# Turning x as pairs of fp16 numbers read as fp32: linear attention with a highway layer on one core

## The chip, the cores and the metric

The kernel runs on one core of a Trainium2 chip. Its time is the device time of one execution in microseconds. The median of three runs of the kernel before is 118.87 us (118.81 to 119.09).

The core's engines each work through a queue of their own, in order: TensorE (PE in the profile; PEld are its weight loads), VectorE (DVE), ScalarE (ACT), GpSimd (POOL) and SyncE (SP), which here issues nearly all transfers. TensorE writes to PSUM only. Semaphores order the engines among each other.

## The reference, cut to what matters

```python
# q, k, v: 8 batches x 8 heads x 576 rows x 64, fp32
q_s = softmax(q, axis=-1)                  # over the 64 features
k_s = softmax(k, axis=2)                   # over the 576 rows
kv  = einsum('bhsd,bhse->bhde', k_s, v)    # 64 x 64 for each batch and head
x   = einsum('bhsd,bhde->bhse', q_s, kv)   # then to 4608 rows x 512
H   = maximum(x @ w_h, 0)
T   = 1 / (1 + exp(-(x @ w_t + b_t)))
out = T * H + (1 - T) * x                  # 4608 x 512, fp32
```

## The kernel before, in words

Rows of x are worked in 36 tiles of 128 rows by 512 columns. Two batches make nine tiles: four of each batch alone, and one that holds the last 64 rows of both. Every step of every tile is a small function, and a long list of step names (`ORDER`) written by hand fixes the order in which they are recorded; each engine's queue is that list cut down to its own instructions. A suffix of a step picks its engine (D VectorE, A ScalarE, P GpSimd).

The steps for a batch: load k, v, q; exponentials of k and q in fp16 (`ek`, `eq`, ScalarE); v to fp16 (`vc`); `kv` multiplies k by v for all heads, and `kr`, `kn` divide by the sums; `qt` turns the exponentials of q on TensorE, and `qc` copies them out of PSUM (`qd` turns those of the last batch by DMA).

The steps for a tile i:

- `xu` (L361): q by kv on TensorE, with the row sums, into PSUM.
- `rs`, `x` (L370, L376): VectorE takes reciprocals and writes x, scaled, as fp16 into SBUF (tile x16, 128 x 512).
- `xt` (L384): TensorE turns x into PSUM, because the next matmuls need its columns on the partitions. Here x is the loaded weight and an identity moves through. Four turns of 128 x 128 fp16; turn n takes every second column of a block of 256, so that n = 2c + r holds the columns 256c + 2p + r, p being the partition. The weights w_h and w_t are loaded in the same arrangement of rows (`load_w`).
- `xe` (L391): VectorE or ScalarE copies the turned x, 512 fp16 numbers a partition, into tile xT in SBUF.
- `mh` (L419) and `mt` (L411): four matmuls each of 512 columns; a quarter of xT is the loaded weight, and w_h (halved, less the identity) or w_t moves through. `bw` puts the bias into the gate's PSUM first, by ScalarE (L399) or by a matmul (L401).
- `th` (tanh on ScalarE, L433 and L435), `dd` (L439), `uu` (L453 on VectorE, or L450 and L451 on GpSimd), `oo` (L471, GpSimd) and `st` (store) finish the tile.

Three tiles (0, 4 and 5) go through the first of these steps in two halves; the last tile's gate goes in two halves of columns. The turned x has one place in PSUM, `turned` (one bank, of which the first half is used), so the turns of one tile wait for the copy of the tile before. The same bank, read as fp32 under the name `spare`, is written by the `fill` matmuls (L167) that keep TensorE busy in the first 17 us. `idf` and `idh` are identities in fp32 and fp16; `idf` is there today, since it is taken off w_h.

Of the kernel before, what the change touches and what calls it, by code (L numbers as in the profile page):

```python
# [8 lines left out]
FP32 = mybir.dt.float32  # L9
FP16 = mybir.dt.float16  # L10
# [55 lines left out]
def kernel(  # L66
# [10 lines left out]
    nc = tc.nc  # L77
    B, H, S, D = q.shape
    DM = H * D
    P = 128  # L80
# [12 lines left out]
    xtp = pool("xtp", 3)  # L93
# [10 lines left out]
    idf = consts.tile([P, P], FP32, name="idf")  # L104
    idh = consts.tile([P, P], FP16, name="idh")
    w16 = {w: consts.tile([P, KC, DM], FP16, name="w16" + w) for w in "th"}
# [8 lines left out]
    turned = ps_xt.tile([P, 2, 4, P], FP16, tag="xtps", name="turned")  # L115
    spare = turned.rearrange("p a c d -> p (a c d)").bitcast(FP32)
    T = {}

    def once(name, make):
        if name not in T:  # L120
            T[name] = make()
        return T[name]
# [10 lines left out]
    def heads(i, k):  # L133
        return (k, k + 1) if i in HALVED else (0, 2)
# [6 lines left out]
    def columns(i, h):  # L141
        return slice(PIECES[h], PIECES[h + 1]) if i == LAST else slice(0, DM)

    def gate(i, h):
        return f"tps{i}_{h}" if i == LAST else f"tps{i}"
# [34 lines left out]
    def load_kv(which):  # L180
        def step(e, b, c):
            n = (2 if which == "k" else 1, 2)[b] if b < 2 else 4
            nc.sync.dma_start(landing(which, b)[:, c:c + n], rows_of(which, b)[:, c:c + n])
        return step
# [193 lines left out]

    def xt(e, i, k):
        k0, k1 = heads(i, k)  # L380
        t = T[f"xtps{i}"] = turned[:, 0]
        for n in range(2 * k0, 2 * k1):
            n0 = n // 2 * 2 * P
            nc.tensor.matmul(t[:, n], T[f"x{i}"][:, n0 + n % 2:n0 + 2 * P:2], idh, is_transpose=True,  # L384
                             start=True, stop=True, skip_group_check=True)

    def xe(e, i, k):
        k0, k1 = heads(i, k)
        t = once(f"xT{i}", lambda: xtp.tile([P, 4, P], FP16, tag="xT", name=f"xT_{i}"))
        copy = nc.vector.tensor_copy if e == "D" else nc.scalar.copy  # L390
        copy(t[:, 2 * k0:2 * k1], T[f"xtps{i}"][:, 2 * k0:2 * k1])  # L391


    def bw(e, i, h=0):
# [8 lines left out]
    def parts_of(i, k):  # L403
        return range(2 * k, 2 * k + 2) if i in HALVED else range(4)

    def mt(e, i, k):
        cs = columns(i, k)
        parts = parts_of(i, k)
        first = once(f"mt{i}", lambda: k) == k and len(parts) < 4
        for n in parts:  # L410
            nc.tensor.matmul(T[gate(i, k)][:, cs], T[f"xT{i}"][:, n], w16["t"][:, n, cs], start=False,  # L411
                             stop=(n == parts[-1] and not first), skip_group_check=True)

    def mh(e, i, k):
        first = f"gps{i}" not in T
        t = once(f"gps{i}", lambda: ps_g.tile([P, DM], FP32, tag="gps", name=f"gps_{i}"))
        parts = parts_of(i, k)
        for n in parts:
            nc.tensor.matmul(t, T[f"xT{i}"][:, n], w16["h"][:, n], start=(first and n == parts[0]),  # L419
                             stop=(n == parts[-1] and not (first and len(parts) < 4)), skip_group_check=True)  # L420


# [50 lines left out]
    def st(e, i, h):  # L473
# [22 lines left out]
        k=load_kv("k"), v=load_kv("v"), q=load_q, w=load_w, b=load_b, bp=bp, bc=bc,  # L496
        wtc=wt_cast, whc=wh_cast, whd=wh_less_identity, ek=ek, vc=vc, kv=kv, kr=kr, kn=kn, eq=eq, qt=qt, qc=qc, qd=qd,
        xu=xu, rs=rs, x=x, xt=xt, xe=xe, bw=bw, mt=mt, mh=mh, th=th, dd=dd, uu=uu, oo=oo, st=st)
    with tc.manual_schedule():
        for step in ORDER.split():  # L500
            name, _, eng = step.partition(":")
# [32 lines left out]
```

## Time and profile before

| | |
|---|---|
| median of the runs | 118.87 us |
| span of the profiled execution | 116.9 us |
| between the two | 2.0 us |
| mean granted TensorE clock | 0.995 |
| HBM read, written | 30.41 MB, 9.44 MB |

The profiled execution's time is known as its span, from the first to the last instruction; the median of the runs counts what lies around it too. In the profile a row of a group reads: line, engine, operation, output and inputs by the program's names, shapes, count; then busy time and the mean of one in ns; then the idle time of the engine just before them, and what ended it. A matmul's record holds its whole passage through the array, and records of matmuls that follow each other overlap; their spacing is read from the chain of waits, which takes each piece from where the one before it ends. The chain goes back from the last instruction, at each step to what released it.

### The profile page before, as it was taken

The page shows a single profiled execution, that of the slowest core. Times are in us where ns is not written, and L with a number is a line of the kernel's source. Part 1 is how long each engine was busy: PE and PEld are TensorE (multiplying, and loading weights), DVE is VectorE, ACT ScalarE, POOL GpSimd, SP SyncE. Part 2 cuts the span into 40 slices and gives each one's busy share as a digit, 9 for nine tenths or more (in the row PEclk, how much of TensorE's full clock was granted, in tenths as well). Part 3 has the DMA queues.
Part 4 walks back from the last instruction along what each step waited for, and adds up shares of the span by engine and source line. Part 5 has one row for each costly group of instructions (what it writes and reads, how often), then busy time and mean ns, then how long its engine had stood idle before and what let it go on. Part 6 is the DMA issues. An engine that isn't in the chain of part 4 may idle for free.

```text
span 116.9 us, 3424 instructions
## 1 busy us (share of the span) xinstructions
PE 109.5 (94%) x1351; PEld 61.6 (53%) x1351; DVE 93.3 (80%) x222; ACT 90.0 (77%) x132; POOL 89.1 (76%) x99
## 2 busy tenths in 40 slices
PE   5999987999999999999999999999999999999930
PEld 2354544545665656565665547566564555554520
DVE  5642587589799979979889798988989887899870
ACT  4356461897999999989999999998597998545520
POOL 5022237208996999999999999999989699999960
PEclk9999999999999999999999999999999999999998
DMA  2999999999999999999999999999999956992875
GB/s 42 399 392 377 408 398 385 375 377 379 393 391 397 383 391 393 358 375 387 357 376 360 387 392 363 390 381 383 399 398 217 302 204 270 397 404 115 315 295 179
DMA packets 24195, 40.58 MB, mean 347 GB/s; under 512 B 5362, under 2 KB 11762, under 8 KB 24180
## 3 DMA queue, kind: packets, MB, share of 16 engines
q1 hardware_dynamic: 24032, 40.24, 96.9%
q8 instruction: 10, 0.16, 0.6%
q10 hardware_dynamic: 148, 0.14, 0.4%
q14 instruction: 5, 0.04, 0.1%
HBM read 30.41 MB, written 9.44 MB: 341 GB/s over the span
## 4 chain that ended last, share of the span: by engine, by line
PE 67%; POOL 15%; issue 6%; DVE 5%; DMA 3%; SPq 1%; POOLq 0%; DVEq 0%
PE tps L411 18%; PE gps L419 16%; PE turned L167 9%; POOL o L471 7%; PE xu L361 6%; PE turned L384 5%; PE kv L269 5%; PE qps L324 4%; POOL u L451 4%; DMA out_dram<-o 3%; POOL g L450 2%; PE qps L319 2%; POOL v L259 2%; DVE x L376 2%; PE tps L401 1%
## 5 line engine op out<-in xcount | busy, mean ns | idle before, releaser
L471 POOL TENSOR_TENSOR o<-u,x 128x512 f32<-128x512 f16 (+1 forms) x36 | 40.6, 1143 | 1.6 <-DVE u L453 0.7
L411 PE MATMUL tps<-w16t,xT 128*128 128x512 f16 (+1 forms) x148 | 37.3, 373 | 0.0
L419 PE MATMUL gps<-w16h,xT 128*128 128x512 f16 x144 | 36.8, 379 | 0.5 <-DVE xT L391 0.5
L376 DVE TENSOR_TENSOR x<-xu,rs 128x512 f16<-128x512 f32 (+1 forms) x39 | 25.2, 649 | 2.4
L259 POOL CAST v<-v 128x1152 f16<-128x1152 f32 (+1 forms) x14 | 14.0, 1010 | 14.7 <-DMA v<-in_v_dram 13.7
L439 DVE SCALAR_TENSOR_TENSOR d<-x,gps 128x512 f16<-128x512 f16 x36 | 24.5, 680 | 0.3
L451 POOL TENSOR_TENSOR u<-g,d 128x512 f16<-128x512 f16 x17 | 19.7, 1158 | 1.7 <-DVE rs L370 0.4
L253 ACT ACTIVATE ek<-k 128x576 f16<-128x576 f32 (+2 forms) x15 | 17.9, 1225 | 3.0 <-DMA k<-in_k_dram 3.0
L419 PEld LDWEIGHTS <-xT 128*128 128x128 f16 x144 | 13.0, 98 | 12.3 <-DVE xT L391 1.8
L399 ACT COPY tps<-ball 128x512 f32<-128x512 f32 x28 | 16.6, 597 | 3.5 <-DVE u L453 3.2
L411 PEld LDWEIGHTS <-xT 128*128 128x128 f16 x148 | 13.2, 98 | 10.6 <-DVE xT L391 0.4
L361 PE MATMUL xu<-kvb,eq 128*128 128x130 f16 (+1 forms) x160 | 14.8, 224 | 0.2 <-DVE kvb L287 0.2
L384 PE MATMUL turned<-idh,x 128*128 128x128 f16 x144 | 14.2, 220 | 0.5 <-DVE x L376 0.5
L391 DVE COPY xT<-turned 128x512 f16<-128x512 f16 (+1 forms) x28 | 10.9, 391 | 4.2 <-PE turned L384 3.0
L435 ACT ACTIVATE tps<-tps 128x512 f32<-128x512 f32 (+1 forms) x20 | 11.2, 559 | 3.6 <-PE tps L411 3.3
L453 DVE SCALAR_TENSOR_TENSOR u<-tps,d 128x512 f16<-128x512 f32 (+1 forms) x19 | 12.7, 671 | 1.4 <-ACT tps L435 0.6
L361 PEld LDWEIGHTS <-eq 128*128 128x128 f16 (+1 forms) x160 | 10.0, 100 | 7.3 <-DVE x L376 2.5
L167 PE MATMUL turned<-blank 128*128 128x512 f16 x40 | 12.4, 458 | 1.5 <-POOL blank L149 1.3
L384 PEld LDWEIGHTS <-x 128*128 128x128 f16 x144 | 9.8, 98 | 6.0 <-DVE x L376 2.1
L307 ACT ACTIVATE qe<-q 128x1024 f16<-128x1024 f32 (+3 forms) x9 | 9.4, 1052 | 4.1 <-DMA q<-in_q_dram 4.1
L450 POOL TENSOR_SCALAR g<-th 128x512 f16<-128x512 f16 x17 | 10.6, 621 | 0.9 <-ACT th L433 0.9
L433 ACT ACTIVATE th<-tps 128x512 f16<-128x512 f32 x17 | 10.0, 594 | 0.9 <-PE tps L411 0.9
(48 smaller groups left out, 106.8 us busy)
## 6 DMA issues: line engine op xcount, KB each, us to landing
k<-in_k_dram SPq DMA_DIRECT2D x6, 1152.0 KB, 12.2
v<-in_v_dram SPq DMA_DIRECT2D x6, 1152.0 KB, 12.0
out_dram<-o SPq DMA_DIRECT2D x23, 256.0 KB, 4.0
q<-in_q_dram SPq DMA_DIRECT2D x10, 512.0 KB, 11.5
out_dram<-o SPq DMA_DIRECT2D x6, 512.0 KB, 3.8
k<-in_k_dram SPq DMA_DIRECT2D x4, 576.0 KB, 9.3
q<-in_q_dram SPq DMA_DIRECT2D x2, 1152.0 KB, 14.2
q<-in_q_dram SPq DMA_DIRECT2D x2, 640.0 KB, 10.5
```

Of the source, the lines that this page charges most:

```text
L167: nc.tensor.matmul(spare, blank[:, 0:P], blank, start=True, stop=True, skip_group_check=True)
L253: nc.scalar.activation(t[:, :, c:c + n].rearrange("p j c d -> p c j d"), T[f"k32{b}"][:, c:c + n].rearrange("p c (j d) -> p c j d", j=NJ), ...
L259: copy(v16[b % NV][:, c:c + n, :, 0:D], T[f"v32{b}"][:, c:c + n].rearrange("p c (j d) -> p c j d", j=NJ))
L361: nc.tensor.matmul(dst, turned_q(b, jp, n), kvb[b % NKV][:, hh, kk], start=True, stop=True, skip_group_check=True)
L376: nc.vector.tensor_mul(t[:, k0:k1], sums(i, k)[:, :, :, 0:64], T[f"rs{i}_{k}"][:, 0:k1 - k0].unsqueeze(3).to_broadcast([P, k1 - k0, 4, D]))
L384: nc.tensor.matmul(t[:, n], T[f"x{i}"][:, n0 + n % 2:n0 + 2 * P:2], idh, is_transpose=True, start=True, stop=True, skip_group_check=True)
L399: nc.scalar.copy(t[:, cs], ball[:, cs])
L411: nc.tensor.matmul(T[gate(i, k)][:, cs], T[f"xT{i}"][:, n], w16["t"][:, n, cs], start=False, stop=(n == parts[-1] and not first), skip_gro ...
L419: nc.tensor.matmul(t, T[f"xT{i}"][:, n], w16["h"][:, n], start=(first and n == parts[0]), stop=(n == parts[-1] and not (first and len(part ...
L439: nc.vector.scalar_tensor_tensor(t, T[f"x{i}"], -0.5, T[f"gps{i}"], op0=ALU.mult, op1=ALU.max)
L451: nc.gpsimd.tensor_mul(t, g, T[f"d{i}"])
L471: eng.tensor_add(t[:, cs], T[f"u{i}_{h}"][:, cs], T[f"x{i}"][:, cs])
```

## The change

The 128 x 512 fp16 numbers of x are read as 128 x 256 fp32 elements, each a pair of neighbours. Two turns of 128 x 128 such elements, with the fp32 identity, take the place of four turns. In the turned tile a partition then holds, for each row of x, the two numbers of a pair side by side: xT gets the shape partition, block c, row, r in place of partition, n, row. The copy moves the same 512 numbers a partition in order. The matmuls L411 and L419 load as weight every second element of a block (`turned_x`), and the weights that move through stay as they are. The list of steps is not changed. After the change, lines behind `xe` are four higher.

```diff
     def xt(e, i, k):
         k0, k1 = heads(i, k)
-        t = T[f"xtps{i}"] = turned[:, 0]
-        for n in range(2 * k0, 2 * k1):
-            n0 = n // 2 * 2 * P
-            nc.tensor.matmul(t[:, n], T[f"x{i}"][:, n0 + n % 2:n0 + 2 * P:2], idh, is_transpose=True,
+        T[f"xtps{i}"] = turned[:, 0].rearrange("p n t -> p (n t)").rearrange("p (c t r) -> p c t r", c=2, r=2)
+        pairs, turned_pairs = T[f"x{i}"].bitcast(FP32), spare[:, 0:2 * P].rearrange("p (c t) -> p c t", c=2)
+        for c in range(k0, k1):
+            nc.tensor.matmul(turned_pairs[:, c], pairs[:, c * P:(c + 1) * P], idf, is_transpose=True,
                              start=True, stop=True, skip_group_check=True)
 
     def xe(e, i, k):
         k0, k1 = heads(i, k)
-        t = once(f"xT{i}", lambda: xtp.tile([P, 4, P], FP16, tag="xT", name=f"xT_{i}"))
+        t = once(f"xT{i}", lambda: xtp.tile([P, 2, P, 2], FP16, tag="xT", name=f"xT_{i}"))
         copy = nc.vector.tensor_copy if e == "D" else nc.scalar.copy
-        copy(t[:, 2 * k0:2 * k1], T[f"xtps{i}"][:, 2 * k0:2 * k1])
+        copy(t[:, k0:k1].rearrange("p c t r -> p (c t r)"),
+             T[f"xtps{i}"][:, k0:k1].rearrange("p c t r -> p (c t r)"))
+
+    def turned_x(i, n):
+        return T[f"xT{i}"][:, n // 2, :, n % 2]
...
-            nc.tensor.matmul(T[gate(i, k)][:, cs], T[f"xT{i}"][:, n], w16["t"][:, n, cs], start=False,
+            nc.tensor.matmul(T[gate(i, k)][:, cs], turned_x(i, n), w16["t"][:, n, cs], start=False,
...
-            nc.tensor.matmul(t, T[f"xT{i}"][:, n], w16["h"][:, n], start=(first and n == parts[0]),
+            nc.tensor.matmul(t, turned_x(i, n), w16["h"][:, n], start=(first and n == parts[0]),
```

## Prediction

> **What bounds the kernel now.** I read the page's shares first, then three stretches of the span, then the chain of waits, then groups by shape.
>
> ```profile
> span 116.9 us, 3424 instructions
> PE 109.5 (94%) x1351; PEld 61.6 (53%) x1351; DVE 93.3 (80%) x222; ACT 90.0 (77%) x132; POOL 89.1 (76%) x99
> ```
>
> The median of the runs shown is 118.87 us, so 2.0 us lie around the span. TensorE is the fullest engine, but a share over the whole span hides the stages:
>
> ```profile
> 24.00:83.00 59.00, 58.99 (x849) 34.98 (x847) 52.05 (x122) 56.31 (x78) 54.12 (x55) 1.00 1.06 381
> 83.00:112.00 29.00, 28.99 (x286) 16.11 (x283) 25.58 (x53) 20.45 (x36) 26.09 (x26) 1.00 0.89 302
> 112.00:117.00 5.00, 0.09 (x1) 0.00 (x0) 1.31 (x4) 0.43 (x2) 1.43 (x2) 0.89 0.55 199
> ```
>
> Columns: the stretch, its length, busy time of PE, weight loads, DVE, ACT, POOL, granted clock, DMA share, GB/s. From 24 to 112 us TensorE leaves 0.02 of 88 us unrecorded, at clock 1.00. Records of matmuls overlap, so that alone does not make it the bound. The chain of waits does, since it gives the spacing of one group after another:
>
> ```profile
> 45.20 0.45 PE qps L324 x8
> ...
> 48.69 0.71 PE kv L269 x69
> 49.40 0.55 PE qps L324 x8
> 49.95 0.86 PE gps L419 x4
> 50.82 0.23 PE xu L361 x4
> 51.05 0.22 PE turned L384 x4
> 51.27 0.86 PE tps L411 x4
> ```
>
> Start, duration, what. Each piece begins where the last one ends: TensorE follows TensorE, with nothing between. Four turns of x (L384) take 0.22 us, 55 ns each; four 512-column matmuls take 0.86 us, 215 ns each. The spacing is about 0.42 ns a column, (215-55)/(512-128). This runs so from 24 to 83 us. After that the chain as drawn goes over POOL and DVE, but POOL is idle for 2.9 of 29 us there and TensorE for none, so I count TensorE as the bound up to its last matmul:
>
> ```profile
> 111.05 1.04 PE L411 MATMUL tps<-w16t,xT 128*128 128x256 f16 x8
> ...
> 113.46 0.50 SPq L479 DMA_DIRECT2D out_dram<-o  x1
> ```
>
> What follows the last matmul (tanh, two VectorE steps, the store and its landing: about 4.8 us) does not change. Loads arrive in time: in the waits from 28 to 50 us a transfer is named once, and from 50 us on no compute engine waits for one.
>
> ```profile
> ACT qe L307 <- DMA q<-in_q_dram: 0.6, 1, 0.6
> ```
>
> **The change, part by part.** Rows of the turn, of its evacuation and of the nearest loads:
>
> ```profile
> L384 PE MATMUL turned<-idh,x 128*128 128x128 f16 x144 | 14.2, 220 | 0.5 <-DVE x L376 0.5
> L384 PEld LDWEIGHTS <-x 128*128 128x128 f16 x144 | 9.8, 98 | 6.0 <-DVE x L376 2.1
> ...
> L391 DVE COPY xT<-turned 128x512 f16<-128x512 f16 x23 | 9.5, 413 | 2.7 <-PE turned L384 1.5 <-ACT tps L435 0.7
> L324 PEld LDWEIGHTS <-qe 128*128 128x128 f16 x80 | 5.2, 98 | 2.0 <-ACT qe L307 0.6
> L361 PEld LDWEIGHTS <-eq 128*64 128x64 f16 x32 | 1.0, 109 | 1.5 <-DVE x L376 1.0 <-issue 0.4
> L411 PEld LDWEIGHTS <-xT 128*128 128x128 f16 x148 | 13.2, 98 | 10.6 <-DVE xT L391 0.4
> ```
>
> *Removed.* 144 fp16 turns with their weight loads, four a tile. The 220 ns of a record is latency; the price on TensorE is the 55 ns of spacing, so 36 tiles x 0.22 = 7.9 us. The chain's own count is lower:
>
> ```profile
> by line: PE tps L411 18.0%; PE gps L419 16.4%; PE turned L167 9.1%; POOL o L471 7.4%; issue 5.9%; PE xu L361 5.7%; PE turned L384 5.2%; PE kv L269 4.6%; PE qps L324 4.0%; POOL u L451 3.6%; DMA out_dram<-o 2.6%; POOL g L450 2.1%; PE qps L319
> ```
>
> 5.2% of 116.9 is 6.1 us of turns on the path. The rest lies in the start-up, or after 83 us where the chain is drawn elsewhere.
>
> *Added.* 72 turns of fp32 elements, two a tile, each one weight load and one matmul that moves 128 columns of the fp32 identity. No matmul of fp32 stands in this trace, so its spacing is unknown. From below: 55 ns, since it moves as many columns as the turn it replaces. From above by bytes: 128 fp32 elements are what 256 fp16 elements are, and eight 256-column matmuls at 111.05 us take 1.04 us with the last one's record of about 0.27 us, so (1.04-0.27)/7 = 110 ns. From further above: 215 ns, a 512-column matmul, if each element were taken in four pieces. I take 55: over all the rows the spacing follows the columns, whatever the tile holds.
>
> The Trainium skill, "FP8 and Floating Point Precision", section TensorE Precision Notes, says that true FP32 takes four passes through the array. Its page "TensorE: Matmul & The Clock Gate", section Terms, says that the transpose mode is four times faster for FP32. By the two together a turn would cost 55 ns, by the first alone 220; no run so far shows either.
>
> *The longer load.* Loads of 128 fp16 columns take 98 ns and loads of only 64 columns 109 ns, so there are two kinds, and the narrow kind is the slower one per column. If an fp32 load is of the slower kind it takes between 109 ns (no more than 64 columns) and 218 ns (twice that). The part above 98 is covered where a 215 ns matmul runs ahead of the turn and x is ready; it shows where the turn waits for x. Of the 36 tiles some 22 begin with such a wait; I put 0.03 us on each, between 0.01 (109-98) and 0.12 (218-98): 22 x 0.03 = 0.6 us, bounds 0.2 to 2.6.
>
> The skill's page on TensorE, section Weight-path perf modes, rules out the fast weight load for FP32 and speaks against the change. With its figure of columns/1.2 a 128-column load would be an estimated 107 ns and could not hide behind a 55 ns turn; the pair would then take some 160 ns, and half of the gain would go.
>
> *Waits.* The order on every engine is the same but for the turns. Four tiles whose first weight load waited for x, and whose matmul waited for the previous copy out of `turned`, get both waits ahead of the load. The load can no longer go early there: below 4 x 0.1 us, within the term just named. Behind it stand the tile's gate or highway matmuls, which need xT anyway.
>
> *Strided weights.* L411 and L419 now load every second element of xT. L384 does this today, at 98 ns and 55 ns spacing, the same as L324, which loads neighbours. So 292 loads change at no cost. If that cover failed (a load longer than the matmul before it), 215 ns matmuls still stand between; below zero it cannot go, since nothing is removed.
>
> *The copy.* L391 reads and writes 512 fp16 elements in a row as before: 413 ns, unchanged. It can start 0.11 us sooner after x, a gain already in the turns.
>
> **Sum.** Half of the 6.1 us on the path, less the loads: -3.05 + 0.6 = -2.4 us. Bounds of the gain's first term: 84 of the turns start between 24 and 83 us and 132 after 24 us, 21 and 33 tiles, at 0.11 us a tile 2.3 and 3.6 us.
>
> ```profile
> 24.00:83.00 59.00, 8.15 (x84) 5.68 (x84) 1.00 1.06 381
> 83.00:117.00 34.00, 4.50 (x48) 3.00 (x45) 0.98 0.84 287
> ```
>
> The profiled span goes from 116.9 to 114.5; with 2.0 around it, 116.5 us.
>
> **Rivals.**
> - *A switch of element type drains the array* (slower). In the chain above, the eight turns that follow kv take 0.55 us, the same eight elsewhere 0.45: changing the shape of the array's tile costs 0.10 us. If going to fp32 and back did the same, or the load could not be laid in behind a running matmul, a tile would pay 2 x 0.10 and save 0.11: +0.09 x 33 = +3.0, +0.6 for loads, so 122.5 us. It decides from 0.055 us a switch on. Against it: fp16 turns and matmuls that write fp32 follow each other today without a gap.
> - *An fp32 column takes twice the time* (bytes bind): 2 x 110 = 220 ns a tile, nothing saved, the loads lost: 118.9 + 0.0 to 0.9, about 119.3 us.
> - *Four pieces an element*: 2 x 215 = 430 ns a tile, +0.21 x 33 + 0.6 = +7.5: 126.4 us. The count of one load and one matmul a turn speaks against it.
> - *Another engine takes the bound.* ACT is busy for 56.3 of 59 us up to 83, and DMA shows a share of 1.06, no room. Half of the gain is lost where ACT's order is tight: about 117.7 us. Against it: ACT's records overlap by about 0.1 us each, as the starts of its instructions show, so 78 of them leave more room than 2.7 us.
>
> ```profile
> 43.64 0.37 ACT L333 COPY eq<-qps 128x256 f16<-128x256 f16 x1
> ...
> 43.89 0.61 ACT L399 COPY tps<-ball 128x512 f32<-128x512 f32 x1
> ```
>
> - *The change doesn't do what it says* (turns in fact hidden): 118.9.
>
> **How the numbers follow.** Forecast 0.42; ACT or the slow load takes half 0.10; twice the time 0.15; drain 0.22; four pieces 0.08; nothing 0.03. A measurement of this kernel tells 0.3% (0.36 us) from no change. Faster: 0.42 + 0.08 = 0.50. Same: 0.03 + 0.02 + 0.04 = 0.09. Slower: 0.11 + 0.22 + 0.08 = 0.41. The likeliest case's own range is 115.3 (3.6 us gained) to 117.7. For eight in ten it must reach into the drain case, up to 122.8.
>
> **What would show it.** Right: L384 with 72 matmuls of f32, two of them 0.11 us in the chain, TensorE's last matmul near 109.7 us, POOL and ACT above 95% in the middle. Wrong: a piece of two turns at or above 0.22 us; a first matmul after a turn that starts 0.1 us late (drain); loads of x above 150 ns with matmuls waiting behind; or turns at 0.11 us with the end unmoved, which would mean another engine was the bound.

## The result and the profile after

| | before | after |
|---|---|---|
| median of the runs, us | 118.89 (118.51 to 119.38, 20 runs) | 119.29 (119.08 to 119.69, 20 runs) |
| ratio to before | | 1.0037 (95%: 1.0026 to 1.0048) |
| span of the profiled execution, us | 116.9 | 117.9 |

The change makes the kernel slower by 0.4 us. The profiled execution of after was the slowest of its 20 (119.69 us), so its span overstates the loss.

The groups of the page of after, in the columns used before:

```profile
L384 PE MATMUL turned<-idf,x 128*128 128x128 f32 x72 | 14.6, 282 | 0.9 <-ACT xT L391 0.5
L384 PEld LDWEIGHTS turned<-idf,x 128*128 128x128 f32 x72 | 8.4, 141 | 6.4 <-DVE x L376 1.7
```

The count is as forecast, 72 turns and 72 loads of fp32. A load takes 141 ns where one of fp16 took 98, and a turn's record 282 where it was 220. What a turn occupies stands in the chain of waits:

```profile
42.87 0.32 PE xu L361 x4
43.19 0.22 PE turned L384 x2
43.41 1.73 PE gps L423 x8
45.14 0.24 PE xu L361 x4
45.38 0.22 PE turned L384 x2
45.59 0.45 PE qps L324 x8
46.04 0.86 PE tps L415 x4
...
47.14 0.22 PE turned L384 x2
...
52.53 0.11 PE qps L324 x2
52.64 0.40 PE turned L384 x2
53.04 0.24 PE xu L361 x4
...
57.88 0.42 PE xu L361 x8
58.31 0.37 PE turned L384 x2
58.67 0.86 PE tps L415 x4
```

Two turns take 0.22 us, as four did before: 110 ns each in place of 55. Nothing is saved. And in some tiles they take more: 0.40 us at 52.64, 0.37 at 58.31. The same places in the chain of before:

```profile
46.74 0.22 PE turned L384 x4
...
52.25 0.30 PE turned L384 x4
...
57.81 0.33 PE turned L384 x4
```

They had 0.30 and 0.33 there. From 46.74 to 57.81 us 11.07 us passed before; after, from 47.14 to 58.31, it is 11.17, and the tile at 52.64 is the 0.10. The stretch from 24 to 83 us does 809 matmuls with TensorE as full as before, while ScalarE and GpSimd have a little less to do in it; nobody else has become the bound:

```profile
24.00:83.00 59.00, 58.95 (x809) 34.76 (x801) 51.76 (x121) 55.60 (x77) 53.96 (x54) 1.00 1.06 381
83.00:112.00 29.00, 28.99 (x261) 16.12 (x260) 25.40 (x54) 20.98 (x36) 25.73 (x26) 1.00 0.85 291
```

The spread of the records, line L384 alone from 24 us to the end (shortest, median and longest, in ns), tells which turns show their load: a record is 272 where the load is covered and up to 329 where it is not, so an uncovered load shows by about 55 ns.

```profile
L384 PE MATMUL turned<-idf,x x64: 272/273/329, 28.2 to 110.0; 128*128 128x128 f32 x64
```

Before, the same view of the fp16 turns shows the two ends close together:

```profile
L384 PE MATMUL turned<-idh,x x128: 218/219/233, 27.9 to 109.1; 128*128 128x128 f16 x128
```

The reading at this point (theory A): the turns cost the same as before, and the loss is the load that shows in the tiles whose first turn has to wait for x and has no running matmul to hide behind. There are twelve (2, 3, 4, 5, 14, 15, 21, 22, 25, 28, 30, 34) by the spacing of their turns: in them the next matmul starts 136 to 166 ns behind the first turn, in every other tile 127 ns behind it or less, mostly 109 to 114. The trace of before already told these tiles apart: there the record of the first turn is 225 to 233 ns in all of them but tile 2, and 218 or 219 in every other tile. Rivals were the stepped weights of L415 and L423, a chance shift of the loads at the start, and a cost of the type itself in every tile.

### The profile page after: what moved, and what is told of

Its sections match the earlier page's. It is cut to its first block, busy times and chain, and to the rows that moved or that the text cites. A ratio compares the mean times of both kernels' runs of the same rounds, so it can differ in the third digit from the quotient of the medians.

```text
span 117.9 us, 3284 instructions
## 1 busy us (share of the span) xinstructions
PE 109.9 (93%) x1279; PEld 61.8 (52%) x1279; DVE 93.5 (79%) x222; ACT 89.9 (76%) x132; POOL 89.1 (76%) x99
## 4 chain that ended last, share of the span: by engine, by line
PE 75%; DMA 15%; DVE 2%; ACT 2%; SPq 2%; issue 0%; DVEq 0%
PE tps L415 25%; PE gps L423 24%; DMA k<-in_k_dram 10%; PE turned L384 8%; PE xu L361 7%; DMA v<-in_v_dram 5%; PE kv L269 5%; PE qps L324 3%; PE qps L319 2%; SPq L183 1%; ACT ek L253 1%; PE tps L405 1%; DVE u L457 1%; DVE d L443 1%; ACT tps L439 1%
## 5 line engine op out<-in xcount | busy, mean ns | idle before, releaser
L415 PE MATMUL tps<-w16t,xT 128*128 128x512 f16 (+1 forms) x148 | 37.3, 373 | 0.0
L423 PE MATMUL gps<-w16h,xT 128*128 128x512 f16 x144 | 36.8, 379 | 0.5 <-DVE xT L391 0.5
L423 PEld LDWEIGHTS <-xT 128*128 128x128 f16 x144 | 13.3, 98 | 12.4 <-DVE xT L391 1.7
L415 PEld LDWEIGHTS <-xT 128*128 128x128 f16 x148 | 13.9, 99 | 10.8 <-DVE xT L391 0.4
L403 ACT COPY tps<-ball 128x512 f32<-128x512 f32 x28 | 16.5, 596 | 3.7 <-DVE u L457 3.6
L384 PE MATMUL turned<-idf,x 128*128 128x128 f32 x72 | 14.6, 282 | 0.9 <-ACT xT L391 0.5
L361 PEld LDWEIGHTS <-eq 128*128 128x128 f16 (+1 forms) x160 | 10.5, 101 | 7.6 <-DVE x L376 2.5
L167 PE MATMUL turned<-blank 128*128 128x512 f16 x40 | 11.9, 444 | 1.5 <-POOL blank L149 1.3
L384 PEld LDWEIGHTS turned<-idf,x 128*128 128x128 f32 x72 | 8.4, 141 | 6.4 <-DVE x L376 1.7
L454 POOL TENSOR_SCALAR g<-th 128x512 f16<-128x512 f16 x17 | 10.6, 622 | 0.9 <-ACT th L437 0.9
```

Source lines behind the costliest of these rows:

```text
L361: nc.tensor.matmul(dst, turned_q(b, jp, n), kvb[b % NKV][:, hh, kk], start=True, stop=True, skip_group_check=True)
L384: nc.tensor.matmul(turned_pairs[:, c], pairs[:, c * P:(c + 1) * P], idf, is_transpose=True, start=True, stop=True, skip_group_check=True)
L403: nc.scalar.copy(t[:, cs], ball[:, cs])
L415: nc.tensor.matmul(T[gate(i, k)][:, cs], turned_x(i, n), w16["t"][:, n, cs], start=False, stop=(n == parts[-1] and not first), skip_group_ ...
L423: nc.tensor.matmul(t, turned_x(i, n), w16["h"][:, n], start=(first and n == parts[0]), stop=(n == parts[-1] and not (first and len(parts) ...
```

## The experiments

### Twelve tiles back to fp16, and weights without steps

The first kernel turns those twelve tiles as before, the others as fp32 pairs:

```diff
+    FOURS = (2, 3, 4, 5, 14, 15, 21, 22, 25, 28, 30, 34)
...
+        if i in FOURS:
+            t = T[f"xtps{i}"] = turned[:, 0]
+            for n in range(2 * k0, 2 * k1):
+                n0 = n // 2 * 2 * P
+                nc.tensor.matmul(t[:, n], T[f"x{i}"][:, n0 + n % 2:n0 + 2 * P:2], idh, is_transpose=True,
...
```

> The twelve tiles whose fp32 turn had nothing ahead to hide its weight load (2, 3, 4, 5, 14, 15, 21, 22, 25, 28, 30, 34) go back to four fp16 turns; the other 24 keep two fp32 turns. Theory A (an fp32 turn holds TensorE for 109 ns, two as long as four fp16 turns, and its load shows by some 55 ns where nothing covers it, so only the uncovered tiles lose): the loss of 12 x 0.04 us goes, the 24 others gain 0.005 us each: 118.8 us, ratio to before 0.998 to 1.001. Theory D (the loss is in something every tile pays, the stepped weight loads or the copy): two thirds of the loss stays, 119.15 us, ratio 1.002 to 1.003.

Measured: 118.95 us (118.62 to 119.08), ratio to before 1.0002 (0.9992 to 1.0012). Its chain of waits, where L387 is the fp16 turn and L393 the fp32 turn:

```profile
46.71 0.22 PE turned L393 x2
...
52.22 0.30 PE turned L387 x4
...
57.78 0.33 PE turned L387 x4
```

The distance from 46.71 to 57.78 is 11.07 us again, as before. To within 0.1% all of the loss lies in the twelve tiles; in the other 24 two fp32 turns and four fp16 turns cost the same. The second kernel keeps the change but loads neighbouring elements of xT as weights (so the columns of x meet the wrong rows of w):

```diff
-        return T[f"xT{i}"][:, n // 2, :, n % 2]
+        return T[f"xT{i}"].rearrange("p c t r -> p (c t r)")[:, n * P:(n + 1) * P]
```

> The changed kernel, but L415 and L423 load neighbouring elements of xT as weight instead of every second one; xT itself is unchanged, so the highway and gate matmuls get columns in the wrong order. Theory A: stepped loads cost nothing, time as the changed kernel, ratio to before 1.003 to 1.005 (119.3 us). Theory C (the stepped loads, 99 ns in place of 98 over 292 loads, take what the turns save): back to before or below, ratio 0.997 to 1.001 (118.8 us).

Measured: 119.28 us, ratio 1.0040 (1.0025 to 1.0055), the same as after, and the loads of L415 and L423 take 99 and 98 ns in both. Stepped weights cost nothing. The changed kernel was also profiled a second time:

> The changed kernel unaltered, for a second profile and a ratio on another chip run. The two profiled spans differ by 1.0 us, the medians by 0.40. If 0.6 us of the spans' difference is chance in the start (k landed later, a chain of DMA k, ACT ek, ACT xT at 21 us), the span here is 117.0 to 117.6 us and the ratio 1.003 to 1.005; if the late start belongs to the change, 117.9 us again.

119.27 us, ratio 1.0041 (1.0026 to 1.0055), span 117.7 us. This profiled execution, too, was a long one (119.52 us, 0.25 above its median), so the two spans of the changed kernel both overstate the loss, and what the start has to do with it stays open. The medians agree: 0.40 and 0.47 us above before.

### What a column of fp32 costs

To take the price of a column apart from that of an instruction, each turn was cut to 64 rows of x, so only 64 columns of the identity move (half of each tile of x stays unturned):

```diff
-            nc.tensor.matmul(turned_pairs[:, c], pairs[:, c * P:(c + 1) * P], idf, is_transpose=True,
+            nc.tensor.matmul(turned_pairs[:, c, 0:64], pairs[0:64, c * P:(c + 1) * P], idf[0:64, 0:64], is_transpose=True,
```

> The changed kernel with each fp32 turn cut to the first 64 rows of x: the same 128 weight columns, but 64 moving columns; the other half of xT holds old numbers. What counts is the spacing from the first turn of a tile to the second, where the first one's load was covered (109 ns in the changed kernel). Theory A (the moving columns go at half speed): about 56 ns. Theory B1 (the load is the bound of the pair, 109 ns for 128 columns): 107 to 109 ns. Theory B2 (load and matmul of fp32 do not overlap, 53 + 53 ns): about 80 ns. The time of the whole says little, since the cut array shape costs 0.10 us at each change.

Measured once: 122.46 us, 3.2 above after. The spacing from the first turn to the second was 110 to 114 ns, and it did not settle the question, because going from 128 rows of the array to 64 and back laid the load bare and cost time of its own (3.2 us over some 33 tiles, 0.1 us each, although half of the columns were gone). The records of line L384 tell more:

```profile
L384 PE MATMUL turned<-idf,x x64: 222/271/275, 28.4 to 112.7; 64*128 64x64 f32 x64
```

The shortest record is 222 ns for 64 columns, and 272 for 128 in the row of after: (272-222)/64 = 0.78 ns a column. The fp16 rows of before, 220 ns for 128 columns and 379 for 512, give (379-220)/384 = 0.41. An fp32 column goes through at about half the speed. That the time is not in the loads (theories B1 and B2) shows in the chain of after: at 45.38 us the first turn's load is covered, and what follows the second turn is fp16, so that only one fp32 load falls in between. If that load were the bound, or could not overlap with a turn of some 55 ns, the fp16 matmul would start about 0.16 us behind the first turn; it starts 0.21 us behind it, two turns of 109 ns. Next, every turn was made twice, which adds work that needs nothing new:

```diff
-        for c in range(k0, k1):
+        for c in [c for c in range(k0, k1) for _ in range(2)]:
```

> The changed kernel with every fp32 turn made twice, so 144 turns; the result is the same. It prices a turn by itself. Theory A: 36 tiles x 0.22 = 7.9 us more on TensorE, of which the part after 24 us (33 tiles, 7.2 us) reaches the end: 126 to 127 us. If a turn costs 55 ns and what was lost is waits alone: 36 x 0.11 = 4.0 us, at most 123.3 us.

Measured: 125.89 us, ratio 1.0592 (1.0570 to 1.0615), just under what theory A gave and well above the 123.3 of its rival. The chain of this kernel shows the price of a turn once more, four in 0.44 us:

```profile
53.73 0.44 PE turned L384 x4
54.17 0.86 PE tps L415 x4
```

72 turns of 0.11 us are 7.9 us of TensorE; the time grew by 125.89-119.29 = 6.6 us, so 84% of added TensorE time reaches the end. Last, the turn as an ordinary fp32 matmul by the identity, with the transpose mode off:

```diff
-            nc.tensor.matmul(turned_pairs[:, c], pairs[:, c * P:(c + 1) * P], idf, is_transpose=True,
+            nc.tensor.matmul(turned_pairs[:, c], pairs[:, c * P:(c + 1) * P], idf,
```

> The changed kernel with the same fp32 operands, but as ordinary fp32 matmuls by the identity and not in transpose mode (two loads and two matmuls for each turn in the built program; the pairs' low bits need not come through). If each of the two goes at the 109 ns of theory A, a tile takes 0.44 us in place of 0.22: +7.2 us, 126.5 us. If an ordinary fp32 pass goes a column as fast as fp16 (55 ns), two of them equal one turn: 119.3 us. If each pass is four times the fp16 price: 134 us.

Measured: 127.00 us, ratio 1.0686 (1.0668 to 1.0704). Its groups and its chain:

```profile
L384 PE MATMUL turned<-idf,x 128*128 128x128 f32 x144 | 23.7, 286 | 0.5 <-DVE x L376 0.5
L384 PEld LDWEIGHTS turned<-idf,x 128*128 128x128 f32 x144 | 20.0, 191 | 4.5 <-DVE x L376 1.5 <-ACT xT L391 0.5 <-DVE xT L391 0.2
```

```profile
53.38 0.50 PE turned L384 x4
```

Each ordinary fp32 turn became two loads and two matmuls: 144 of both where 72 were written, 0.50 us for a tile (0.44 plus the part of a load that nothing covers). So the transpose mode halves the price of fp32. The Trainium skill, "TensorE: Matmul & The Clock Gate", section Terms, gives it a factor of four for FP32; here it is two, and the fp32 turn stays at half the rate of fp16.

### If the turns had been cheaper: one turn left out

Would a saving have reached the end at all? In the 33 whole tiles the second turn was left out (half of x is not turned there). That takes 33 x 0.11 = 3.6 us off TensorE, as much as the upper bound of the gain in the forecast.

```diff
-        for c in range(k0, k1):
+        for c in range(k0, k1 if i in HALVED else k0 + 1):
```

> The changed kernel with the second fp32 turn left out in the 33 tiles that are turned whole; the copy and all else stay, and half of each such xT holds old numbers. It gives TensorE what the prediction expected of 55 ns turns: 33 x 0.11 = 3.6 us less. If TensorE sets the pace and six to nine tenths of a saving reach the end (theory A, and the prediction's sum): 2.2 to 3.2 us under the changed kernel, 116.1 to 117.1 us. If another engine or the transfers would take the bound (the prediction's rival): at most 1.2 us gained, 118.1 us or more.

Measured: 118.55 us (118.34 to 118.77), ratio 0.9966 (0.9954 to 0.9979): 0.7 us below after, where more was expected. Two engines were then relieved in turn. With GpSimd's step g (L454) left out as well, so that u lacks the 1 that is added to tanh:

```diff
-            g = dp.tile([P, DM], FP16, tag="g16", name=f"g16_{i}")
-            nc.gpsimd.tensor_scalar(g, T[f"th{i}"], 1.0, 1.0, op0=ALU.add, op1=ALU.mult)
-            nc.gpsimd.tensor_mul(t, g, T[f"d{i}"])
+            nc.gpsimd.tensor_mul(t, T[f"th{i}"], T[f"d{i}"])
```

> The kernel with the second fp32 turn left out, and GpSimd freed too: its step g = tanh + 1 (L454, 17 times, 10.6 us) is left out, so u = tanh times d in these 17 tiles. With one turn left out alone TensorE had 3.6 us less to do and the end came only 0.7 us sooner than in the changed kernel. Theory P (GpSimd, 19.4 of 20 us busy from 40 to 80 us, held the end back): the end follows TensorE now, 1.3 to 2.4 us further, 116.1 to 117.3 us. Theory T (transfers, ScalarE or the waits between TensorE and VectorE hold it): at least 118.2 us.

> The control: the changed kernel with both its turns, and the same step of GpSimd left out. If TensorE alone sets the pace of the changed kernel, freeing GpSimd gives next to nothing: 118.8 to 119.3 us. If GpSimd holds the end by itself, it falls as far as in the run beside it, to 117.5 us or less.

118.50 us with one turn (ratio 0.9970, 0.9955 to 0.9986), 119.31 with both (1.0036, 1.0021 to 1.0052): no help. With ScalarE's bias copies (L403) left out, and then also q of batch 2 not loaded (batch 1's is used for both):

```diff
-            nc.scalar.copy(t[:, cs], ball[:, cs])
+            BARE.add(i)
...
-            nc.tensor.matmul(T[gate(i, k)][:, cs], turned_x(i, n), w16["t"][:, n, cs], start=False,
+            nc.tensor.matmul(T[gate(i, k)][:, cs], turned_x(i, n), w16["t"][:, n, cs],
+                             start=(i in BARE and T[f"mt{i}"] == k and n == parts[0]),
```

```diff
+        if b == 2:
+            T["q322"] = T["q321"]
+            return
```

> One fp32 turn a tile left out, and ScalarE freed: the 28 copies of the bias into the gate's PSUM (L403, 16.5 us) are left out, the gate's first matmul starts the sum instead. The chain of the run with GpSimd freed went over a late v (landing at 37.7 us) and over ScalarE from 52 to 58 us, not over TensorE. Theory S (ScalarE holds the middle): a further 0.5 to 1.5 us, 117.0 to 118.0 us. Theory L (the loads up to 38 us alone): 118.2 to 118.6 us, nothing more.

> The same, and the loads eased too: q of batch 2 (1152 KB, some 3 us of transfers) is not loaded, batch 1's is used in its place. If loads and ScalarE together are what held TensorE's saving back, the end now follows TensorE: below the control beside it (both turns, same easing) by 2.2 us or more of the 3.6. If what holds it lies in the waits between TensorE and VectorE from tile to tile, the two differ by 1 us or less, as the changed kernel and the one-turn kernel do (0.7 us).

> The control: the changed kernel with both turns, the bias copies left out and q of batch 2 not loaded. If TensorE sets its pace, only the start (up to 38 us) can gain: 118.0 to 119.2 us.

118.66 us (ratio 0.9978, 0.9952 to 1.0005) with the copies left out; 118.54 (0.9974, 0.9952 to 0.9996) with the load too; the control with both turns 119.43 (1.0039, 1.0018 to 1.0060). In the three relieved kernels with one turn TensorE's last matmul lies within 0.2 us of where the one-turn kernel alone has it, so neither GpSimd's g, nor the bias copies, nor that load holds the saving back by itself. What was left was to compare the ends of the traces. TensorE's last eight matmuls and the last store's issue, from the timelines of after and then of the one-turn kernel:

```profile
112.05 1.04 PE L415 MATMUL tps<-w16t,xT 128*128 128x256 f16 x8
...
114.51 0.38 ACTq L483 DMA_DIRECT2D out_dram<-o  x1
```

```profile
109.90 1.04 PE L415 MATMUL tps<-w16t,xT 128*128 128x256 f16 x8
...
112.53 0.54 SPq L483 DMA_DIRECT2D out_dram<-o  x1
```

TensorE ends 2.1 us sooner, but from the last issue to the end of the span it takes 117.0-112.5 = 4.5 us in place of 117.9-114.5 = 3.4. The transfers of the one-turn kernel from 112 to 117 us show what lasts longer (GB/s in 40 slices of 0.125 us), and from 110 to 113 us what came before:

```profile
GB/s 426 295 148 33 0 33 0 33 147 328 410 360 360 377 312 377 344 328 361 328 222 41 33 16 25 25 16 25 25 0 0 0 0 0 0 0 0 0 0 0
```

```profile
q8 instruction: 1, 0.02, 2.6%
```

After the last stores (0.31 to 0.41 TB/s until 114.5 us) a trickle of some 25 GB/s goes on for 1.0 us, about what one of sixteen DMA engines moves when all together move 381: one engine is still at work. It was behind already before these stores: from 112.4 to 113.0 us the slices show 33 or 0 GB/s, one 4 KB packet at a time. Just before, from 110.8 to 112.0 us, a packet of the instruction queue was under way, for 2.6% of 16 engines x 3 us = 1.2 us. The three relieved kernels with one turn show the same: a packet that starts at 109.6 to 110.9 us, and 4.3 to 4.5 us from the last issue to the end. The queue has ten packets of 16 KB (0.16 MB) in the span and is read here as the one that brings TensorE's next instructions. With 66 instructions fewer the tenth packet falls among the last stores; in after it comes at 106 us. The test: give the one-turn kernel the 66 instructions back where they cost nothing, by cutting the first 11 fillers of 512 columns into four each; and the reverse, 32 fillers cut in the changed kernel, to bring a packet into its tail.

```diff
+    CUT, fills = 11, []
+
     def fill(e, n):
         for _ in range(n):
-            nc.tensor.matmul(spare, blank[:, 0:P], blank, start=True, stop=True,
-                             skip_group_check=True)
+            fills.append(1)
+            w = P if len(fills) <= CUT else DM
+            for c in range(0, DM, w):
+                nc.tensor.matmul(spare[:, c:c + w], blank[:, 0:P], blank[:, c:c + w], start=True, stop=True,
+                                 skip_group_check=True)
```

> One turn a tile left out in the 33 whole tiles (so the second half of x stays unturned there), and 11 of the first 13 fillers of 512 columns cut into four of 128: the same time on TensorE at the start, 66 instructions more, as many as the left-out turns are. Theory F (a fetch of instructions that falls among the last stores holds one of their DMA engines for about 1 us): the fetch moves out of the tail, from the last store's issue to the end takes 3.4 us as in the changed kernel in place of 4.3 to 4.5, and the time is 117.3 to 117.9 us, 1.4 to 2.0 under the changed kernel's 119.29. Rival S (the stores that now come closer together end no sooner, whatever the instruction queue does): 118.4 to 118.7 us as with the turn left out alone, and a tail of 4.3 us.

> The changed kernel with both turns, and the first 32 fillers of 512 columns cut into four of 128: the same time on TensorE, 192 instructions more, which puts a fetch (one in 256 instructions) where the one-turn kernel has it. Theory F: a packet of the instruction queue falls at 111 to 113 us, the tail grows from 3.4 to about 4.4 us, and the time is 120.0 to 120.5 us, where the changed kernel alone has 119.29. Rival S: 119.1 to 119.5 us with the tail at 3.4 us. If the cut fillers themselves cost time, the last matmul comes later too, and the tail alone counts.

The one-turn kernel with cut fillers: 117.64 us (117.35 to 118.01), ratio 0.9888 (0.9870 to 0.9907), 0.9 below the same kernel without them. Its last matmuls, its last issue, its transfers from 112 to 116 us (slices of 0.1 us) and its packet between 104 and 112 us:

```profile
110.14 1.04 PE L420 MATMUL tps<-w16t,xT 128*128 128x256 f16 x8
...
112.59 0.38 ACTq L488 DMA_DIRECT2D out_dram<-o  x1
```

```profile
GB/s 430 389 348 348 430 82 0 0 0 0 143 307 369 328 348 389 451 318 287 348 379 318 348 348 348 195 21 0 0 0 0 0 0 0 0 0 0 0 0 0
```

```profile
q8 instruction: 1, 0.02, 0.7%
```

TensorE ends no sooner than without the cut (110.14 against 109.90), the trickle is gone, and the span ends at 116.0, 3.4 us behind the last issue. The packet lies at 105.1 us now. So the additional time behind the last store, about 1 us, went with the packet. That the packet held up the one engine is argued from the order of the two; the traces don't name the engine of a packet.

The reverse did not succeed. The changed kernel with 32 fillers cut took 119.97 us (ratio 1.0086, 1.0070 to 1.0101). Its profile is of an execution of 122.16 us with a mean granted clock of 0.975; there the eleventh packet came 4 us ahead of the last store's issue, and the tail was 3.4 us. Four more tried to place it better, by other numbers of cut fillers (27, 11, 31 and 30):

> The changed kernel with both turns, and the first 27 fillers cut into four: 162 instructions more, so a packet of the instruction queue falls some 1.5 us later than with 32 fillers cut, about 2 us ahead of the last store. Theory F: from the last store's issue to the end it takes about 4.4 us in place of 3.4, and the time is 119.9 to 120.5 us. Rival (the packet costs only where a turn is left out, or the cut fillers are what costs): a tail of 3.4 us, and 119.1 to 119.6 us if the fillers cost nothing.

> The changed kernel with both turns and the first 11 fillers cut into four, as in the one-turn kernel of g1: 66 instructions more, no packet of the instruction queue in the last 10 us. Theory F, and cut fillers that cost nothing: 119.1 to 119.5 us, a tail of 3.4 us, and the one-turn kernel of g1 is 1.5 to 1.9 us faster than this. If cut fillers cost time by themselves: 119.7 us or more, and the last matmul later than 112.9 us.

> The changed kernel with both turns, and the first 31 fillers cut into four: 186 instructions more. If an eleventh packet of the instruction queue is fetched at 112.5 to 114.5 us, theory F expects 4.0 to 4.5 us from the last store's issue to the end in place of 3.4, and 0.5 to 1.0 us more than the kernel of 162 more instructions (119.67 us), so 120.1 to 120.7. If it is not fetched, a tail of 3.4 us and 119.4 to 119.8 us. If it is fetched there and the tail stays at 3.4 us, theory F doesn't hold for this kernel.

> The same with the first 30 fillers cut: 180 instructions more. The same conditions: with a packet among the last stores a tail of 4.0 to 4.5 us and 120.1 to 120.7 us; without one a tail of 3.4 us and 119.4 to 119.8 us.

| fillers cut | packets of the queue | median, us | ratio to before |
|---|---|---|---|
| 11 | 10 | 119.45 | 1.0044 (1.0020 to 1.0068) |
| 27 | 10 | 119.67 | 1.0052 (1.0026 to 1.0077) |
| 30 | 10 | 120.03 | 1.0100 (1.0071 to 1.0130) |
| 31 | 10 | 120.19 | 1.0125 (1.0084 to 1.0165) |

None of the four has an eleventh packet, and all have a tail of 3.4 us; the expected tail of 4 us and more was not produced. The cut fillers cost up to 0.9 us by themselves when many are cut, which was not expected and was not followed up; that, and not the packet, may be the 0.7 us of 32 cut ones. With 11 cut, as in the one-turn kernel, the cost is at most 0.2 us, so the comparison above stands, with the 11-cut kernel as its control: 119.45-117.64 = 1.8 us of the 3.6 us left out reach the end. Part of the other half shows as idle time, in the stretches of the one-turn kernel with cut fillers:

```profile
24.00:83.00 59.00, 58.41 (x799) 33.32 (x792) 52.47 (x124) 56.85 (x78) 53.81 (x54) 1.00 1.06 381
83.00:112.00 29.00, 27.93 (x248) 14.51 (x246) 26.05 (x54) 20.54 (x37) 27.24 (x28) 1.00 0.92 314
```

TensorE idles for 0.59 us up to 83 us. Of the 1.07 us behind it 0.82 lie after the last matmul, which ends at 110.14 + 1.04 = 111.18 us, so 0.25 are left: 0.84 us in all, 0.06 in after. A matmul's record (mostly 220 to 380 ns) is longer than its spacing, so shorter waits don't show as idle time; they may hold the rest. The longest three rows of the waits of that kernel's weight loads from 24 to 112 us are

```profile
PEld L366 <- DVE x L381: 3.1, 9, 0.6
PEld L274 <- ACT ek L258: 1.4, 3, 0.5
PEld L366 <- DVE kvb L292: 1.3, 3, 0.6
```

Loads idle without harm while a matmul runs, so these sums are larger than TensorE's own idle time. In after the same three rows are 2.5, 0.4 and 1.1 us, so no single row carries the difference. VectorE was not relieved in any run, and which of the chains sets the pace was not told apart.

## Why the prediction was wrong, step by step

- *The bound.* Right as far as the forecast used it: TensorE follows TensorE up to 112 us, and 84% of the TensorE time added by double turns reached the end. It does not hold in the other direction over several us: of 3.6 us taken away half reached the end. So "half of the 6.1 us on the path" would have been too much even with turns of 55 ns; the rival in which other engines keep half of the gain describes that, though neither relief of ScalarE nor of GpSimd returned it.
- *The turn: the step that failed.* "I take 55: over all the rows the spacing follows the columns, whatever the tile holds." It is 109 to 110 ns, the middle one of the three bounds, the one by bytes. All the rows that the step rested on were of 16-bit numbers, so they could not tell columns from bytes. The term of -3.05 us was 0 (the tiles with covered loads cost the same in both kernels). The rival that had the two-fold column, "about 119.3 us", names the mechanism and the outcome, 119.29; it had a chance of 0.15.
- *The load.* Right in kind: 141 ns, inside the bounds of 109 and 218, and it shows only where no matmul covers it. It shows by about 55 ns on ten tiles, and on two more together with the waits of the next point, rather than by 30 on 22. The first fp16 load showed there too, by up to 14 ns (233 against 219 in the rows above), so such a tile loses 56-14 = 42 ns and ten lose 0.4 us, 0.6 with the two others; the forecast had 0.6, and the medians differ by 0.4. That the sum came so close is in part luck: the price was set too low and the number of tiles too high.
- *The waits moved ahead of the load.* The tile at 52.64 us is one of the four: 0.10 us more, at the bound that was set. A second one (tile 30) loses 0.10 us as well, the other two 0.01 us or nothing. The sum stayed within the load's term.
- *Stepped weights and the copy* at nothing: right. The weights cost nothing by experiment, and the copy is where it was:

```profile
L391 DVE COPY xT<-turned 128x512 f16<-128x512 f16 x23 | 9.5, 413 | 3.4 <-PE turned L384 2.8 <-ACT tps L403 0.4
```

- *The other rivals.* A switch of type drains nothing: in the rows at 45.38 the fp16 matmuls start 0.21 us behind the first of the two turns. A switch of the array's shape does, as the cut to 64 rows showed. Four pieces an element (215 ns a turn) fell for the transpose mode, at 109 ns; the ordinary fp32 matmul does cost that much, two matmuls of 112 ns for one turn. On weight loads the Trainium skill, "TensorE: Matmul & The Clock Gate", section Weight-path perf modes, spoke against the change with its rule that FP32 gets no fast load. The trace agrees with the rule, 141 against 98 ns, and it is felt in the uncovered tiles alone.
- *The range* of 115.3 to 122.8 us held the time; the side was wrong.

## What to carry to other kernels

A 32-bit column is not the price of a 16-bit column: before trading four 16-bit instructions for two of 32 bits, look for a row with 32-bit data, and if there is none, let the bound by bytes carry as much weight as the one by columns. Count, for a longer load, only the places where nothing runs ahead of it to cover it; they can be read off one by one, here already from the records of the first fp16 turns in the trace of before, and undoing the change in these alone brought the loss back to zero. When an experiment of "leave it out" gains too little, compare the ends of the two traces before blaming an engine: here about 1 of 1.8 us was lost behind the last store.

## What was not expected of the hardware

- In the transpose mode an fp32 column takes 0.78 ns, an fp16 column 0.41 ns; a turn of 128 x 128 takes 109 ns and 55 ns. The ordinary fp32 matmul of the same size takes two loads of 191 ns and two matmuls spaced 0.11 us.
- Instructions are brought by DMA packets of 16 KB, each under way for 0.9 to 1.9 us in the runs here. The queue is read as TensorE's because 66 more TensorE instructions moved its tenth packet from 110.8 to 105.1 us; that it shares engines with the stores is read from the one engine that was behind after it. The Trainium skill, "Runtime: NRT & Kernel Launch", section Instruction fetch mechanics, has blocks of 16 KiB, 256 instructions each, and calls the crossing of a block mostly hidden. The size agrees (10 packets, 0.16 MB); hidden it was not when the packet fell among the last stores of the one-turn kernels, which then ended about 1 us later.
